# Scores of four heads on two row halves of TensorE, with unpadded pooled k and exponentials over two heads, in a fused pooling attention and MLP kernel

## Chip, cores, metric

One core of a Trainium2 chip. The metric is the device time of one execution in microseconds (us).

## The reference, cut to what matters

```python
# q, k, v: 8 batches, 8 heads, 576 positions, 64 channels
k_p = k.reshape(B, H, 72, 8, 64).mean(axis=3)          # pooled: 72 keys
v_p = v.reshape(B, H, 72, 8, 64).mean(axis=3)
attn = softmax(q @ k_p.T / 8)                          # 576 x 72 a head
x = (attn @ v_p)  -> (B, 576, 512)
u = x + lam * einsum('ts,bsd->btd', w_tok, alpha1 * x + beta1)
out = u + lam * (relu((alpha2 * u + beta2) @ w_ch1) @ w_ch2)   # 512 -> 2048 -> 512
```

The contraction of the scores is only 64 deep, half of TensorE's 128 rows. The last 64 of a head's 576 positions, "the remainder" below, are kept apart from the two halves of 256.

## The kernel before

The rows of all batches go through the MLP in nine blocks of 512. While block n runs on TensorE, the attention of batch n+1 is woven into it by a list of (position, work) pairs: `mlp_A` of hidden chunk j stands at position j (0 to 15), the 16 pieces of `mlp_B` at 16 to 31, and the attention's pieces have fractional positions between them. Every engine executes its share of the list in that order.

Scores are computed transposed (keys on the partitions of PSUM, the buffers that TensorE's matmuls write). `qT` has two sub-rows of 64 channels stacked on 128 partitions, so the kernel before pairs it with a pooled k that is zero in the other half:

```python
    def att_K(b, u, copy):
        # ... pooled k of four heads in ps_kp, 128 partitions (each half a copy) ...
        for a in range(2):
            rows = slice(64 * a, 64 * a + 64)
            (copy or ...)(out=kpT_pool[u][rows, a], in_=kp[rows])   # rest of kpT stays zero

    def att_S(b, h):
        u, r, hh = h // 4, h // 2 % 2, h % 2
        ET = ET_pool[h]
        for half in range(2):
            n0, n = 256 * half, 256 + 64 * half
            ps_sc = gp("ps_sc")                                      # one of 6 general PSUM buffers
            nc.tensor.matmul(out=ps_sc[0:SPG, 0:256], lhsT=kpT_pool[u][:, half, h % 4, :],
                             rhs=st["qT"][u][:, 2 * (h % 4):2 * (h % 4) + 2, :])
            if half:
                nc.tensor.matmul(out=ps_sc[0:SPG, 256:320], lhsT=kpT_pool[u][:, hh, h % 4, :],
                                 rhs=st["rem_qT"][:, :, h // 2::4].rearrange("p c i -> p i c"))
            nc.scalar.activation(out=ET[:, n0:n0 + n], in_=ps_sc[0:SPG, 0:n],
                                 func=AF.Exp, bias=0.0, scale=0.125)

    def att_AV(b, h):      # "AV": five matmuls, then on VectorE
        # ... av = ET[:, m0:m0+128].T @ [vp | 8], rec = 1/av[:, 64], x = av * rec ...

    def mlp_A(n, j):       # "a chunk": four 512-column matmuls, then on ScalarE
        # ... Hj = Relu(w1_j.T @ u + bias) ...
```

and the timetable of batch b from 2 on:

```python
        for h in range(8):
            at = 7.4 + 1.15 * h
            todo.append((at, lambda h=h: att_S(b, h)))         # scores, exponentials
            todo.append((at + 2.0, lambda h=h: att_AV(b, h)))  # two chunks later
```

The softmax here doesn't subtract the row's maximum and nothing guards it: scores larger than these inputs give would overflow.

## Time and profile before

| | kernel before |
|---|---|
| time, median | 364.95 us (3 runs, 364.85 to 365.48) |
| span of the profiled run | 363.5 us |
| TensorE busy | 96% |
| one batch's period in the steady part | 37.08 us |

The period is the mean distance of the first output addition of neighbouring blocks (from 102 to 288 us).

In all views PE is TensorE, PEld its weight loads, DVE VectorE, ACT ScalarE and POOL GpSimd. A line of a timeline gives start and length in us, then engine, source line, names and shapes, and in brackets the idle time before it and who ended it. `ps_s`, `ps_sc` and `ps_r` hold scores (`ps_r` those of the remainder), `ps_h` a chunk of the first MLP layer, `ps_ch` the second layer, `ps_tok` the token mixing.

```profile
L469 PE MATMUL ps_av<-vp,ET 72*128 72x66 f16 x256 | 18.0, 193 | 0.3 <-ACT wtT L299 0.3
L416 DVE CAST kpT<-ps_kp 64x288 bf16<-64x288 f32 x26 | 11.8, 455 | 9.4 <-PE ps_kp L409 5.2
```

TensorE (first figure) is busy for 37.00 of 37.00 us: it never waits. In the group lines the last column is the idle time of the engine just before these instructions, with who ended it; AV waited 0.3 us in the whole kernel, in the setup.

### The profile page before, as it was taken

To read this page: it belongs to the slowest core of one execution; us is meant where nothing else is said; L and a number is where in the kernel's file an instruction comes from. 1 tells how busy PE (TensorE), PEld (TensorE's weight loads), DVE (VectorE), ACT (ScalarE), POOL (GpSimd) and SP (SyncE) were. 2 spreads that over 40 slices of the span, in tenths; PEclk is the share of its full clock that TensorE was granted. 3 is DMA by queue.
4 is the path that set the end of the run, shared out by engine and by line. 5 is a ranking of instruction groups with operands and counts; after the bars stand their busy time and mean duration, and the time that the engine had idled before them with its cause. 6 is when DMAs were issued, how large, how long until landed. Compare 5 with 4: busy or idle time off the path is not lost.

```text
span 363.5 us, 5915 instructions
## 1 busy us (share of the span) xinstructions
PE 348.4 (96%) x2229; PEld 188.7 (52%) x2229; DVE 212.7 (59%) x456; ACT 153.9 (42%) x319; POOL 86.8 (24%) x99
## 2 busy tenths in 40 slices
PE   4888999899999999999999999999999999999994
PEld 1566666355644564456445644565456545545541
DVE  5574176669774878576857786677658761011011
ACT  2562995027800790069005910592049304703700
POOL 8469406252117000620053005300510000000000
PEclk9999999999999999999999999999999999999998
DMA  8999910998959872987198919872810032011012
GB/s 125 203 216 262 216 26 2 160 228 202 142 119 223 153 124 62 244 159 123 51 218 149 156 52 220 171 131 61 215 67 0 31 87 74 0 58 60 1 58 58
DMA packets 65886, 44.58 MB, mean 123 GB/s; under 512 B 32377, under 2 KB 57021, under 8 KB 65858
## 3 DMA queue, kind: packets, MB, share of 16 engines
q1 hardware_dynamic: 50480, 33.30, 38.3%
q0 software_dynamic: 15072, 10.76, 20.5%
q8 instruction: 17, 0.28, 0.3%
q10 hardware_dynamic: 306, 0.14, 0.2%
q14 instruction: 11, 0.09, 0.1%
HBM read 38.30 MB, written 9.44 MB: 131 GB/s over the span
## 4 chain that ended last, share of the span: by engine, by line
PE 90%; DVE 5%; ACT 1%; DMA 1%; issue 1%; ACTq 0%; DVEq 0%
PE ps_h L553 33%; PE ps_ch L571 33%; PE ps_tok L518 12%; PE ps_sc L450 4%; PE ps_av L469 2%; DVE x_tm L477 2%; PE ps_sc L453 1%; DMA vecs<-in_moe_alpha_dram 1%; PE ps_bc L278 1%; DVE kpT L416 1%; PE ps_kp L403 1%; DVE w L339 1%; PE ps_q L368 1%; DVE xs L484 0%; ACT u_fm L539 0%
## 5 line engine op out<-in xcount | busy, mean ns | idle before, releaser
L558 ACT ACTIVATE Hj<-ps_h,bias_cols 128x512 bf16<-128x512 f32 x144 | 98.7, 689 | 154.4 <-PE ps_h L553 153.5
L553 PE MATMUL ps_h<-u_fm,w 128*128 128x512 bf16 (+1 forms) x592 | 138.1, 374 | 1.3 <-ACT u_fm L539 1.1
L571 PE MATMUL ps_ch<-w,Hj 128*128 128x512 bf16 x576 | 134.2, 379 | 0.0
L571 PEld LDWEIGHTS <-Hj 128*128 128x128 bf16 x576 | 55.0, 98 | 62.0
L553 PEld LDWEIGHTS <-w 128*128 128x128 bf16 x592 | 63.4, 114 | 44.9 <-issue 1.8
L576 DVE TENSOR_TENSOR u_sb<-u_sb,ps_ch 128x512 f32<-128x512 f32 x36 | 24.7, 686 | 74.7 <-PE ps_ch L571 74.3
L518 PE MATMUL ps_tok<-xs,wtT 128*128 128x512 bf16 (+1 forms) x200 | 49.6, 379 | 1.8 <-DVE xs L484 1.8
L455 ACT ACTIVATE ET<-ps_sc 72x256 f16<-72x256 f32 (+1 forms) x128 | 44.5, 404 | 2.5 <-PE ps_sc L450 2.2
L520 DVE TENSOR_TENSOR u_sb<-x_tm,ps_tok 128x512 f32<-128x512 f32 (+1 forms) x40 | 27.5, 687 | 30.7 <-PE ps_tok L518 30.7
L477 DVE TENSOR_TENSOR x_tm<-ps_av,rec 128x320 f32<-128x320 f32 x64 | 31.4, 491 | 2.3
L147 POOL CAST rem_q<-rem_raw 128x256 bf16<-128x256 f32 x7 | 3.1, 437 | 123.3 <-DMA rem_raw<-in_q_dram 123.3
L518 PEld LDWEIGHTS <-wtT 128*128 128x128 bf16 (+1 forms) x200 | 19.2, 98 | 25.5 <-DVE xs L484 1.6
L522 DVE TENSOR_TENSOR u_bf<-u_sb,al_bc 128x512 bf16<-128x512 f32 (+1 forms) x38 | 29.0, 763 | 1.4
L438 DVE TENSOR_TENSOR v_u<-v_u 72x512 f32<-72x512 f32 (+1 forms) x48 | 28.3, 589 | 1.2
L450 PE MATMUL ps_sc<-qT,kpT 128*72 128x256 bf16 x128 | 25.4, 275 | 0.5 <-DVE kpT L416 0.4
L475 DVE RECIPROCAL rec<-ps_av 128x5 f32<-128x5 f32 x64 | 12.2, 191 | 18.6 <-PE ps_av L473 17.7
L469 PEld LDWEIGHTS <-ET 72*128 72x128 f16 x256 | 15.9, 98 | 11.9 <-issue 0.5
L162 POOL TENSOR_TENSOR k_raw<-k_raw 128x512 f32<-128x512 f32 x14 | 18.3, 1307 | 15.9 <-DMA k_raw<-in_k_dram 15.9
L164 POOL TENSOR_TENSOR k_bf<-k_raw 128x512 bf16<-128x512 f32 x14 | 19.4, 1386 | 1.1
L484 DVE TENSOR_TENSOR xs<-x_tm,lamal_bc 128x512 bf16<-128x512 f32 x26 | 18.3, 705 | 0.9
L469 PE MATMUL ps_av<-vp,ET 72*128 72x66 f16 x256 | 18.0, 193 | 0.3 <-ACT wtT L299 0.3
L416 DVE CAST kpT<-ps_kp 64x288 bf16<-64x288 f32 x26 | 11.8, 455 | 9.4 <-PE ps_kp L409 5.2
(111 smaller groups left out, 216.5 us busy)
## 6 DMA issues: line engine op xcount, KB each, us to landing
out_dram<-u_sb SPq DMA_DIRECT2D x32, 256.0 KB
k_raw<-in_k_dram SPq DMA_DIRECT2D x14, 512.0 KB
v_u<-in_v_dram SPq DMA_DIRECT2D x12, 512.0 KB
q_bf<-in_q_dram POOLq DMA_DIRECT2D x16, 256.0 KB, 6.7
w<-in_moe_w_ch_dram POOLq DMA_DIRECT2D x8, 512.0 KB, 10.9
v<-in_v_dram POOLq DMA_DIRECT2D x4, 256.0 KB, 6.8
out_dram<-u_sb SPq DMA_DIRECT2D x8, 128.0 KB
rem_raw<-in_q_dram SPq DMA_DIRECT2D x15, 64.0 KB
```

The lines of the kernel that those rows point to most:

```text
L438: nc.vector.tensor_tensor(out=t[:, :, 0:n], in0=t[:, :, 0:n], in1=t[:, :, n:2 * n], op=ALU.add)
L450: nc.tensor.matmul(out=ps_sc[0:SPG, 0:256], lhsT=kpT_pool[u][:, half, h % 4, :], rhs=st["qT"][u][:, 2 * (h % 4):2 * (h % 4) + 2, :])
L455: nc.scalar.activation(out=ET[:, n0:n0 + n], in_=ps_sc[0:SPG, 0:n], func=AF.Exp, bias=0.0, scale=0.125)
L469: nc.tensor.matmul(out=av[:, c, :], lhsT=ET[:, m0:m0 + 128], rhs=vp1[:, hh, :])
L477: nc.vector.tensor_tensor(out=x[:, :, dd:dd + D], in0=av[:, :, 0:64], in1=rec.unsqueeze(2).to_broadcast((P, 5, D)), op=ALU.mult)
L518: nc.tensor.matmul(out=ps_tok, lhsT=wtT[0:kk, at, t0:t0 + P], rhs=xs[0:kk, sc, :], start=(sc == 0), stop=(sc == 4))
L520: nc.vector.tensor_tensor(out=s["u"][p0:p1, :], in0=st1[b]["x"][p0:p1, c, :], in1=ps_tok[p0:p1, 0:DM], op=ALU.add)
L522: eng.tensor_tensor(out=s["u_bf"][p0:p1, :], in0=s["u"][p0:p1, :], in1=al2_bc[p0:p1, :], op=ALU.mult)
L553: nc.tensor.matmul(out=ps_h[:, t0:t1], lhsT=w1_of(cc, j), rhs=u_fm[n][:, cc, t0:t1], start=(cc == 0), stop=(cc == 3))
L558: nc.scalar.activation(out=t, in_=ps_h, func=AF.Relu, bias=bias_cols[:, j:j + 1], scale=1.0)
L571: nc.tensor.matmul(out=ps, lhsT=Hj[n, j][:, 128 * m:128 * m + 128], rhs=w2[j // 4][:, j % 4, :], start=(j == 0), stop=(j == NJ - 1))
L576: nc.vector.tensor_tensor(out=u, in0=u, in1=ps, op=ALU.add)
```

## The change

Its intent: the two halves of the rows hold separate matmuls, one with k on rows 0 to 63 and one on rows 64 to 127, and can run side by side, so that the zeros are no longer multiplied. Four heads form one group with twelve matmuls, into four general PSUM buffers and the two of the MLP output. Pooled k needs one copy without padding in place of two. An exponential then covers a 256-wide half of two heads at once (512 elements in place of 256 or 320). Batch 0 keeps the old form.

```diff
+        if b:
+            copy(out=kp_pool[u], in_=kp)
+            return
...
+    def att_S4(b, u):
+        lo = [psB.tile([P, DM], FP, tag="ch", bufs=2, name="ps_s") for _ in range(2)]
+        hi = [gp("ps_s") for _ in range(2)]
+        r = [gp("ps_r")[0:SPG, 0:128]... for _ in range(2)]
+        for i in range(4):                     # remainders of heads 0..3, halves in turn
+            a = i % 2
+            nc.tensor.matmul(out=r[a][:, i // 2], lhsT=kp[64 * a:64 * a + 64, i, :],
+                rhs=rest[64 * a:64 * a + 64, :, 2 * u + i // 2::4]...)
+        for i in (2, 3, 0, 1):
+            for a in range(2):                 # the pair on the two row halves
+                rows = slice(64 * a, 64 * a + 64)
+                nc.tensor.matmul(out=(hi if i > 1 else lo)[a][0:SPG, 256 * (i % 2):...],
+                    lhsT=kp[rows, i, :], rhs=qT[rows, 2 * i:2 * i + 2, :])
+        def exp(k):      # k = 0, 1: remainders; 2, 3: halves of heads 2, 3; 4, 5: of heads 0, 1
+            ...
...
-        for h in range(8):
-            at = 8.8 + 1.1 * h if first else 7.4 + 1.15 * h
-            lag = 3.3 if first else 2.0
-            todo.append((at, lambda h=h: att_S(b, h)))
-            todo.append((at + lag, lambda h=h: att_AV(b, h)))
...
+        for u in range(2):
+            at = (9.6 if first else 6.3, 12.8)[u]
+            todo.append((at, lambda u=u: att_S4(b, u)))
+            for k, dt in enumerate((0.1, 0.1, 0.2, 1.1, 2.1, 3.0)):
+                todo.append((at + dt, lambda k=k: st1[b]["exp"](k)))
+            lag = 0.9 if first else 0.0
+            for i, dt in ((2, 2.0), (3, 2.6), (0, 4.0), (1, 4.5)):
+                h = 4 * u + i
+                todo.append((at + lag + dt, lambda h=h: att_AV(b, h)))
```

More of the change, by code (lines that the diff above doesn't have):

```diff
@@ L231 @@
     load_wtok()
-    vp1_pool, kpT_pool, ET_pool = [], [], []
+    vp1_pool, kpT_pool, kp_pool, ET_pool = [], [], [], []
     for i in range(4):
@@ L241 @@
             kpT_pool.append(t)
-    for i in range(H):
-        t = const.tile([SPG, S + 64], F16, tag=f"ET_{i}", name=f"ET_{i}")
-        nc.vector.memset(t[:, S:], 1.0)
+            kp_pool.append(const.tile([P, 4, SPG], BF, tag=f"kp_{i}", name=f"kp_{i}"))
+    for i in range(2):
+        t = const.tile([SPG, 4, S + 64], F16, tag=f"ET_{i}", name=f"ET_{i}")
+        nc.vector.memset(t[:, :, S:], 1.0)
         ET_pool.append(t)
@@ L445, in att_S @@
         u, r, hh = h // 4, h // 2 % 2, h % 2
-        ET = ET_pool[h]
+        ET = ET_pool[u][:, h % 4]
         for half in range(2):
@@ L457, in att_S @@
         st["ET"][h] = ET
+    def att_S4(b, u):
+        st = st1[b]
+        qT, kp, rest = st["qT"][u], kp_pool[u], st["rem_qT"]
+        lo = [psB.tile([P, DM], FP, tag="ch", bufs=2, name="ps_s") for _ in range(2)]
+        hi = [gp("ps_s") for _ in range(2)]
+        r = [gp("ps_r")[0:SPG, 0:128].rearrange("p (h i) -> p h i", i=64) for _ in range(2)]
+        for i in range(4):
+            a = i % 2
+            nc.tensor.matmul(
+                out=r[a][:, i // 2], lhsT=kp[64 * a:64 * a + 64, i, :],
+                rhs=rest[64 * a:64 * a + 64, :, 2 * u + i // 2::4].rearrange("p c i -> p i c"))
+        for i in (2, 3, 0, 1):
+            for a in range(2):
+                rows = slice(64 * a, 64 * a + 64)
+                nc.tensor.matmul(
+                    out=(hi if i > 1 else lo)[a][0:SPG, 256 * (i % 2):256 * (i % 2) + 256],
+                    lhsT=kp[rows, i, :], rhs=qT[rows, 2 * i:2 * i + 2, :])
+        ET = ET_pool[u]
+        for i in range(4):
+            st["ET"][4 * u + i] = ET[:, i]
+        def exp(k):
+            if k < 2:
+                o, i = ET[:, k::2, 512:S], r[k]
+            else:
+                a, pair = k % 2, (hi, lo)[k // 2 - 1]
+                h = 2 if k < 4 else 0
+                o = ET[:, h:h + 2, 256 * a:256 * a + 256]
+                i = pair[a][0:SPG, :].rearrange("p (h i) -> p h i", i=256)
+            nc.scalar.activation(out=o, in_=i, func=AF.Exp, bias=0.0, scale=0.125)
+        st["exp"] = exp
     def att_AV(b, h):
@@ L694, in attention @@
                 todo.append((11.0 + 1.2 * u, lambda u=u: first_V(b, u, nc.scalar.copy)))
-        for h in range(8):
-            at = 8.8 + 1.1 * h if first else 7.4 + 1.15 * h
-            lag = 3.3 if first else 2.0
-            todo.append((at, lambda h=h: att_S(b, h)))
-            todo.append((at + lag, lambda h=h: att_AV(b, h)))
-            if h % 2:
-                eng = nc.gpsimd if first and h < 7 else nc.vector
-                todo.append((at + lag + 0.1, lambda h=h, eng=eng: att_X(b, h - 1, h + 1, eng)))
-            elif not first:
-                todo.append((0.2 + 1.0 * h, lambda h=h: att_V(b, h // 2)))
+        for u in range(2):
[7 more added lines that the diff above has]
+                todo.append((at + lag + dt, lambda h=h: att_AV(b, h)))
+                if i % 2:
+                    eng = nc.gpsimd if first and (u, i) != (1, 1) else nc.vector
+                    todo.append((at + lag + dt + 0.1,
+                                 lambda h=h, eng=eng: att_X(b, h - 1, h + 1, eng)))
+        if not first:
+            for hp in range(4):
+                todo.append((0.2 + 2.0 * hp, lambda hp=hp: att_V(b, hp)))
         for c in range(5):
```

## The prediction

> **What bounds the kernel now.** I read the page's busy shares first, then the slices, the groups, and finally the timeline of TensorE and ScalarE in one attention phase.
>
> ```profile
> PE 348.4 (96%) x2229; PEld 188.7 (52%) x2229; DVE 212.7 (59%) x456; ACT 153.9 (42%) x319; POOL 86.8 (24%) x99
> PE   4888999899999999999999999999999999999994
> ACT  2562995027800790069005910592049304703700
> L455 ACT ACTIVATE ET<-ps_sc 72x256 f16<-72x256 f32 (+1 forms) x128 | 44.5, 404 | 2.5 <-PE ps_sc L450 2.2
> L450 PE MATMUL ps_sc<-qT,kpT 128*72 128x256 bf16 x128 | 25.4, 275 | 0.5 <-DVE kpT L416 0.4
> ```
>
> TensorE is the bound: after the first few slices it is never below 9 tenths. ScalarE's 42% is an average that misleads: it is near 9 tenths in the slices where attention of batch b runs beside the first MLP layer of block b-1, and idle elsewhere. That phase is the one that the change rewrites. In it the PE timeline (start, length) of the kernel before reads:
>
> ```profile
> 162.16 0.38 PE L450 MATMUL ps_sc<-qT,kpT 128*72 128x256 bf16 x2
> 162.38 0.24 PE L453 MATMUL ps_sc<-rem_qT,kpT 128*72 128x64 bf16 x1
> 162.46 1.03 PE L553 MATMUL ps_h<-u_fm,w 128*128 128x512 bf16 x4
> 163.33 0.38 PE L450 MATMUL ps_sc<-qT,kpT 128*72 128x256 bf16 x2
> ```
>
> Starts are to be subtracted, as lengths include the pipeline. One head's scores cost 162.46 - 162.16 = 0.30 us of TensorE (two 256-column matmuls 0.11 apart, then 0.075 for the 64 strided columns); one hidden chunk of the MLP (four 512-column matmuls, "a chunk" below) costs 163.33 - 162.46 = 0.87. No idle time is printed here: from 65 us on the records show one TensorE gap above 0.1 us, about 0.4 us at 89 us. So anything removed from PE's stream counts in full, and so does any wait put into it.
>
> The ScalarE timeline of an attention phase:
>
> ```profile
> 87.83 0.69 ACT L558 ACTIVATE Hj<-ps_h,bias_cols 128x512 bf16<-128x512 f32 x1 [0.35 <-PE ps_h L553]
> 88.42 0.69 ACT L455 ACTIVATE ET<-ps_sc 72x256 f16<-72x256 f32 x2
> 89.00 0.69 ACT L558 ACTIVATE Hj<-ps_h,bias_cols 128x512 bf16<-128x512 f32 x1
> ```
>
> A Relu holds the engine 0.58 us (start to next start; 0.69 until its result), the two exponentials of a head 0.58 together. Relu must wait for its chunk: in the records it starts 0.20 to 0.25 us after the next matmul could start on PE. In the kernel before both exponentials of a head follow one Relu, and its attention-value matmuls (AV) come two chunks later, so they never waited.
>
> **What the Trainium skill says.** (1) "TensorE: Matmul & The Clock Gate", Part 3, Packing small matmuls: matmuls on different row groups run side by side, with starts some 4 ns apart. No run yet shows it here; it is the hope of the change. (2) "TensorEngine Tiling (Array Packing)", Key Properties: "Changing tiling mode (not just tile) drains the TensorE". The trace agrees and gives the price, at the places where 32-row weights (L428) come between full ones:
>
> ```profile
> 50.19 0.60 PE L426 MATMUL ps_v<-v,pool_v 128*72 128x256 f16 x4
> 50.72 0.40 PE L428 MATMUL ps_v<-v,pool_vr 32*72 32x256 f16 x2
> 51.05 0.41 PE L450 MATMUL ps_sc<-qT,kpT 128*72 128x256 bf16 x2
> ```
>
> Four 256-column matmuls should take 4 x 0.109 = 0.436 and take 0.53; two should take 0.218 and take 0.33. So in and out of the mode costs 0.09 + 0.11 = 0.20 us. (3) The same page, Gotcha 1: different row tiles must not share a PSUM bank at once; the change gives the halves separate banks, hence four banks and the two of the MLP output per group. (4) "ScalarE: Activation LUTs", What ACT_TABLE_LOAD costs: with immediate scale and bias 186 ns + 0.833 ns an element, neighbours overlapping by 93 ns. The trace has 0.37 us for an uncontended 256-wide exponential, 30 ns less than that; at its slope I estimate 0.59 us for 512 wide, 0.48 of it holding the engine.
>
> **The change, part by part** (batches 1 to 7, so 14 groups of four heads; batch 0 keeps the old form).
>
> 1. *Scores.* Before: 4 x 0.296 = 1.18 us a group. After: the same 12 matmuls, but as pairs on two row halves: two pairs of 0.075, four of 0.109, some 0.03 of skew, plus 0.20 for the mode, 0.82 us. Estimated gain 0.36 x 14 = **5.0 us**. Weight loads should stay hidden: after a mode switch the second 72-column load follows the first by only about 0.03 us.
>
> 2. *k without padding.* One copy of 128x288 on VectorE for two of 64x288 (455 ns each): 14 copies less, but VectorE is not the bound. At most the 0.4 us gap at 89 us goes (there a score matmul waits on this copy). The same group now needs the transposed q remainder about 1 us earlier, in batch 2 just as that transfer lands; I set the two off as zero.
>
> 3. *Exponentials.* Before 8 x 0.58 = 4.6 us of ScalarE per batch. After, per group two of 128 (about 0.16 each) and four of 512 (0.48): 2.24, so 4.5 per batch. No throughput is gained. What changes is order, and there lies the cost. The compiled streams, from batch 2 on, are:
>
> ```
> group 0  PE : S4 h7 h8 AV2 AV3 h9 h10 AV0 AV1
>         ACT: r r e2 Relu7 e3 Relu8 e4 Relu9 e5
> group 1  PE : S4 h13 h14 AV2 h15 AV3 B0 AV0 B1 AV1
>         ACT: r r Relu13 e2 e3 Relu14 e4 Relu15 e5
> ```
>
> (S4: scores of the group; h: a chunk; B: four matmuls of the second layer, as long as a chunk; e2, e3: the two column halves of heads 2 and 3; e4, e5: of heads 0 and 1; r: the remainders.) AV2's second matmul needs e3. Count from S4's end. Group 0: h7 done on PE at 0.87, Relu7 starts at 1.08, e3 at 1.66, its result at 2.25, seen by PE 0.05 later (the records' ScalarE-to-PE delay): 2.30. PE stands at AV2 at 2 x 0.87 + 0.03 = 1.77: **a wait of 0.53**. AV0 has the same pattern with Relu9 and e5: **0.53**. Group 1: e2 from 1.66, e3 from 2.14, result 2.73, 2.78 at PE: **1.0** at AV2; at AV0, with e5 behind Relu15, ready at 5.19 where PE stands at 4.81: **0.4**. Sum 2.5 us a batch, six batches: **+14.9 us**. Each of these was absent before, because an exponential did not stand behind a Relu that had itself to wait for the chunk just before the AV.
>
> 4. *Batch 1* runs on another timetable with 0.9 more lag: AV finds its exponentials ready. The first B takes a PSUM buffer that now holds scores of heads 0 and 1 until e4: +0.6. In return AV of its last head comes some 1.6 chunks earlier, which should take away the wait
>
> ```profile
> 65.44 0.82 PE L518 MATMUL ps_tok<-xs,wtT 128*128 128x512 bf16 x3 [1.11 <-DVE xs L484]
> ```
>
> which is 1.27 us by the starts: -1.2. Net -0.6.
>
> Sum: 364.95 - 5.0 + 14.9 - 0.6 = 374.3; I say **374.0 us**, 2.5% slower.
>
> **Rivals.**
> A. *The waits do not appear and the row halves work*: 364.95 - 5.0 - 1.2, about 359 us. For it: the timetable looks tuned by hand. Against: the instruction order leaves ScalarE idle between e2 and Relu7 while e3's scores lie ready, and PE has only one chunk of 0.87 to cover 0.2 + 0.58 + 0.59 + 0.05 = 1.42 us.
> B. *The halves do not overlap* (shared streaming of q, weight loads in a row, or the waits of their semaphores in between): a group costs 1.18 + 0.20, so +2.8 instead of -5.0; with the waits 382 us, without them 367 us. Nothing in the trace of before shows two row groups together, so this is open; the skill's measurements speak against it.
> C. *PSUM becomes the bound*: four of six general buffers go to one group, so the next chunks wait for Relu or exponentials to empty them. Following the six slots round, each was emptied at least as early as PE comes to it, h7's by about nothing (Relu6 ends as S4 ends). That could add 0.1 to 0.3 us a group, 1 to 4 us.
> D. *ScalarE as a throughput bound*: Relu 16 x 0.58 + 4.5 = 13.8 us in a phase of some 19 us on PE. Not reached; only its order matters.
>
> **Range and chances.** The waits are 24 differences of about 1.4 to 2.7 us against PE times; an error of 0.07 in each moves the sum by 1.7. The scores may be off by 3, C adds up to 4. That gives 366 to 380 as eight in ten. 2% slower is 372.25, 1.75 below the point; with a spread of some 4 and 7% for rival A: slower 0.62, within 2% 0.33, faster 0.05.
>
> **What the profile after would show.** Step 1: starts of the paired 256-column matmuls a few ns to 0.03 apart within a pair and 0.11 between pairs, S4 from start to next chunk near 0.82 (rival B: 1.3). Step 3: PE's idle time before AV with ScalarE's exponential as its releaser, about 2.5 us a batch from batch 2 on, PE's busy share falling to about 90%, and a 512-wide exponential near 0.59 us. Step 4: the 1.1 us wait at the first ps_tok gone. Rival C would show idle time before ps_h instead. I am wrong if AV waits are well under 0.4 us each (a Relu quicker off its chunk, or exponentials much shorter), or if S4 is far from 0.82.

## More of the kernel before

The busy time of the engines in one such period (the columns are the stretch, its length, then busy time and instructions of each engine, in the order PE, PEld, DVE, ACT, POOL, and last the granted clock, the DMA share and GB/s), and the groups for AV and the copies of pooled k:

```profile
160.00:197.00 37.00, 37.00 (x230) 19.83 (x229) 25.68 (x55) 15.31 (x33) 8.14 (x8) 1.00 0.66 139
```

## The result

| | before | changed |
|---|---|---|
| time, median | 365.16 us (4 runs) | 376.42 us (4 runs, 375.81 to 376.69) |
| ratio | | 1.0306, 95% interval 1.0288 to 1.0324 |
| span of the profiled run | 363.5 us | 374.1 us |
| TensorE busy | 96% | 93% |
| a batch's period in the steady part | 37.08 us | 38.79 us |

The ratio here and below is the mean time of one kernel's fast runs over that of the other's in the same rounds, so not quite the ratio of the medians. The change made the kernel 3% slower.

The page of the changed kernel, in the lines that answer to those of before:

```profile
PE 349.4 (93%) x2229; PEld 180.1 (48%) x2229; DVE 205.5 (55%) x438; ACT 151.8 (41%) x289; POOL 87.1 (23%) x99
PE   4988998998999989998999899999999999999994
PE 81%; ACT 10%; DVE 5%; issue 1%; DMA 1%; ACTq 0%; DVEq 0%
L495 ACT ACTIVATE ET<-ps_s 72x512 f16<-72x512 f32 x56 | 32.2, 588 | 0.0
L509 PE MATMUL ps_av<-vp,ET 72*128 72x66 f16 x256 | 20.5, 195 | 10.0 <-ACT ET L495 9.7
```

Between the eighth slice and the last TensorE never fell below 9 tenths before; now it drops to 8 four times there. The chain that ended last, 90% TensorE before, runs for a tenth of the span through ScalarE. And AV, which did not wait before, waits 10.0 us, of which 9.7 are ended by the exponential L495. This idle time is counted from the modelled end of the matmul before; by the starts, which decide, each wait is some 0.17 us longer.

One group of scores and what follows it on TensorE (group 0 of batch 3):

```profile
126.17 0.20 PE L410 MATMUL ps_kp<-pool_rem,rem_k 128*128 128x16 bf16 x2
126.30 0.35 PE L473 MATMUL ps_r<-rem_qT,kp 64*72 64x64 bf16 x4
126.48 0.60 PE L480 MATMUL ps_s<-qT,kp 64*72 64x256 bf16 x8
127.05 1.89 PE L593 MATMUL ps_h<-u_fm,w 128*128 128x512 bf16 x8
128.77 0.20 PE L509 MATMUL ps_av<-vp,ET 72*128 72x66 f16 x1
129.33 0.27 PE L509 MATMUL ps_av<-vp,ET 72*128 72x66 f16 x3 [0.36 <-ACT ET L495]
```

and on ScalarE at the same time:

```profile
126.89 0.42 ACT L495 ACTIVATE ET<-ps_r 72x128 f16<-72x128 f32 x2
127.21 0.59 ACT L495 ACTIVATE ET<-ps_s 72x512 f16<-72x512 f32 x1
128.11 0.69 ACT L598 ACTIVATE Hj<-ps_h,bias_cols 128x512 bf16<-128x512 f32 x1 [0.31 <-PE ps_h L593]
128.69 0.58 ACT L495 ACTIVATE ET<-ps_s 72x512 f16<-72x512 f32 x1
```

The twelve score matmuls take from 126.17 + 0.05 (the two small matmuls before them) to 127.05, 0.83 us for four heads where the kernel before needed 1.18: the part of the change that was its purpose works. But after its first 512-wide exponential ScalarE stands idle for 0.31 us with the next scores ready, because the next instruction in its order is a Relu whose chunk TensorE is only working on. The second exponential starts at 128.69 behind that Relu and ends at 129.27; AV's second matmul, which TensorE could have had at 128.80, starts at 129.33. In the second group of a batch two exponentials stand behind the Relu (batch 2):

```profile
98.27 0.20 PE L509 MATMUL ps_av<-vp,ET 72*128 72x66 f16 x1 [0.40 <-ACT ET L495]
98.75 0.27 PE L509 MATMUL ps_av<-vp,ET 72*128 72x66 f16 x3 [0.28 <-ACT ET L495]
```

By the starts of the matmuls, a batch waits 0.53 and 0.53 us in group 0 and 1.01 (in two steps) and 0.38 in group 1: 2.45 us, equal within 0.01 in all six batches from 2 to 7.

Where the 10.56 us between the two spans come from, by the distance of the blocks' first output additions:

| stretch | attention in it | changed against before |
|---|---|---|
| to the first output of block 0 | batches 0, 1 | +0.10 |
| block 0 to block 1 | batch 2 | +1.89 |
| blocks 1 to 6, five periods | batches 3 to 7 | +1.67, +1.77, +1.67, +1.77, +1.67 |
| after | none | +0.02 |

The timed difference, 11.26 us by the medians, is 0.7 larger than that of the spans: the two profiled executions were timed at 365.27 and 375.81 us, 10.54 apart, and the changed kernel's was the fastest of its four.

### The profile page after: what moved, and what is told of

It is laid out like the page before. It is cut to its first block, busy times and chain, and to the rows that moved or that the text cites.

```text
span 374.1 us, 5840 instructions
## 1 busy us (share of the span) xinstructions
PE 349.4 (93%) x2229; PEld 180.1 (48%) x2229; DVE 205.5 (55%) x438; ACT 151.8 (41%) x289; POOL 87.1 (23%) x99
## 4 chain that ended last, share of the span: by engine, by line
PE 81%; ACT 10%; DVE 5%; issue 1%; DMA 1%; ACTq 0%; DVEq 0%
PE ps_ch L611 31%; PE ps_h L593 28%; PE ps_tok L558 12%; ACT Hj L598 5%; ACT ET L495 4%; PE ps_av L509 2%; PE ps_s L480 2%; DVE x_tm L517 1%; DVE v_u L442 1%; PE ps_bc L279 1%; DMA vecs<-in_moe_alpha_dram 1%; PE ps_r L473 1%; PE ps_kp L404 1%; DVE w L340 1%; PE ps_q L369 1%
## 5 line engine op out<-in xcount | busy, mean ns | idle before, releaser
L593 PE MATMUL ps_h<-u_fm,w 128*128 128x512 bf16 (+1 forms) x592 | 134.2, 374 | 1.6 <-ACT u_fm L579 1.1
L495 ACT ACTIVATE ET<-ps_s 72x512 f16<-72x512 f32 x56 | 32.2, 588 | 0.0
L509 PE MATMUL ps_av<-vp,ET 72*128 72x66 f16 x256 | 20.5, 195 | 10.0 <-ACT ET L495 9.7
L509 PEld LDWEIGHTS <-ET 72*128 72x128 f16 x256 | 14.2, 97 | 25.7 <-ACT ET L495 18.7
L524 POOL TENSOR_TENSOR xs<-x_tm,lamal_bc 128x512 bf16<-128x512 f32 x6 | 9.5, 1591 | 23.6 <-DVE x_tm L517 23.2
L79 POOL DMA_DIRECT2D q_bf<-in_q_dram x16 | 12.4, 776 | 7.6 <-DVE q_bf L78 5.5
```

Of the source, the lines that this page charges most:

```text
L495: nc.scalar.activation(out=o, in_=i, func=AF.Exp, bias=0.0, scale=0.125)
L509: nc.tensor.matmul(out=av[:, c, :], lhsT=ET[:, m0:m0 + 128], rhs=vp1[:, hh, :])
L524: eng.tensor_tensor(out=xs[:, 0:4, cols], in0=x[:, 0:4, cols], in1=lamal_bc[:, cols].unsqueeze(1).to_broadcast((P, 4, D * (h1 - h0))), op= ...
L593: nc.tensor.matmul(out=ps_h[:, t0:t1], lhsT=w1_of(cc, j), rhs=u_fm[n][:, cc, t0:t1], start=(cc == 0), stop=(cc == 3))
```

## The experiments

Theory: the order on ScalarE makes AV wait; the row halves gain what they should; and the first two attention batches lose something of their own. Rivals: ScalarE's throughput or PSUM is the bound, so that a better order would only move the waits; the wide exponentials are to blame; the row halves gain nothing once the change of mode is paid. Each run was correct, and each is compared with runs of the kernel before in the same rounds.

### e1_exp_early: all exponentials ahead of the Relu

```diff
-            for k, dt in enumerate((0.1, 0.1, 0.2, 1.1, 2.1, 3.0)):
+            for k, dt in enumerate((0.1, 0.1, 0.2, 1.1, 2.1, 3.0) if first
+                                   else (0.1, 0.1, 0.11, 0.12, 0.13, 0.14)):
```

> From batch 2 on all six exponentials of a group stand on ScalarE ahead of the next chunk's Relu; nothing else changes. Theory (the order on ScalarE makes AV wait): the four waits of a batch in front of AV, 2.45 us in the trace of the changed kernel, vanish in six batches, so 376.4 - 14.7 = 361.7 us, and the profile shows no TensorE idle with the exponential as releaser from 80 us on. Rival (ScalarE's throughput, or PSUM emptied too late because Relus now come later): the waits move to ps_h and less than half of 14.7 us comes back, 369 us or more.

Measured: 362.62 us, ratio to before 0.9937 (0.9922 to 0.9952). 13.8 of the expected 14.7 us came back. The groups show the waits gone, and ScalarE's timeline the new order:

```profile
L509 PE MATMUL ps_av<-vp,ET 72*128 72x66 f16 x256 | 16.3, 193 | 0.3 <-ACT wtT L300 0.3
L558 PE MATMUL ps_tok<-xs,wtT 128*128 128x512 bf16 (+1 forms) x196 | 49.4, 379 | 2.5 <-DVE xs L524 2.2
```
```profile
161.81 0.42 ACT L495 ACTIVATE ET<-ps_r 72x128 f16<-72x128 f32 x2
162.12 2.05 ACT L495 ACTIVATE ET<-ps_s 72x512 f16<-72x512 f32 x4
164.03 2.63 ACT L598 ACTIVATE Hj<-ps_h,bias_cols 128x512 bf16<-128x512 f32 x4
```

The four 512-wide exponentials hold ScalarE from 162.12 to 164.03, so the next Relu starts about 1 us later than its chunk would allow. Three Relus then follow one another without a gap, 0.57 us from start to start against 0.87 of TensorE for a chunk, and before the fourth ScalarE is already idle for 0.08: the delay is made up without TensorE waiting. The spans differ by 12.85 us. Of the 1.85 that are missing there, some 1.4 us is the second line: in every batch the first token-mixing matmul now waits 0.12 or 0.35 us for VectorE, which the AV waits had hidden; another 0.5 was lost before the first output of block 0, where this edit changes nothing (six traces with the same timetable up to there have that output between 77.76 and 78.49 us, so this is scatter). The period is 36.59 us: 2.20 less than with the change's order, 0.49 less than before. The rival of throughput and PSUM falls: only the order was changed, and no new wait stands at `ps_h`.

### e2_av_later: leave the exponentials, move AV back

```diff
-            lag = 0.9 if first else 0.0
+            lag = 0.9 if first else 1.0
```

> The exponentials stay where the change put them, AV comes one chunk later on TensorE from batch 2 on. Theory: the waits of group 0 vanish (0.53 + 0.53), those of group 1 fall from 1.01 + 0.38 to about 0.15 + 0; but VectorE then has only one chunk left between the last AV and the first token-mixing matmul, which waits some 0.8 us. Per batch 2.45 - 0.15 - 0.8 = 1.5 us back, six batches 9 us: about 367.4 us. Rival (AV waits for something else than the exponential): the same 0.5 us waits in front of AV at its new place, 376 us.

Measured: 374.84 us, ratio 1.0268 (1.0253 to 1.0283); the expectation of 367.4 us was wrong. The waits in front of AV went as expected (none is left in group 0), but:

```profile
104.26 1.24 PE L558 MATMUL ps_tok<-xs,wtT 128*128 128x512 bf16 x5 [0.81 <-DVE xs L524]
...
137.85 1.02 PE L611 MATMUL ps_ch<-w,Hj 128*128 128x512 bf16 x4 [0.76 <-ACT ET L495]
```

The second line first: the first matmul of the second MLP layer takes a PSUM buffer that holds scores of heads 0 and 1 until the fifth exponential, which stands behind two Relus. With AV moved back, this matmul came earlier on TensorE, and waits 0.92 us by the starts; I had not counted it. The token mixing (first line) waits 0.98 and 1.21 us in turn by the starts, where 0.8 was expected. So the late exponential reaches TensorE by another way. Moving the consumer only moved the wait; moving the producer removed it.

### e3_exp_narrow: the change's order with 256-wide exponentials

```diff
-            nc.scalar.activation(out=o, in_=i, ...)                     # 72 x 2 x 256
+            for j in range(2):                                          # from batch 2 on
+                nc.scalar.activation(out=ET[:, h + j, 256 * a:256 * a + 256],
+                                     in_=pair[a][0:SPG, 256 * j:256 * j + 256], ...)
```

> From batch 2 on the 512-wide exponentials of two heads are taken apart into two of 256, at the same places in ScalarE's order. Theory (order, not width): an AV needs only its own head's half, ready about 0.2 us sooner, but the second half holds up the other head, so each batch's 2.45 us fall by about 0.4, six batches 2.7 us: 373.7 us. Rival (the wide exponential is what makes AV wait): most of the 14.7 us come back, 365 us or less. Other rival (two at once saves ScalarE time that matters): slower than 376.4 us.

Measured: 373.85 us, ratio 1.0236 (1.0219 to 1.0253), against 373.7 expected. Width is not the cause; two heads at once even costs 2.6 us in this order, as AV gets its own head's half later (with 256-wide exponentials it waits 0.43 us in group 0 by the starts, in place of 0.53).

### e9_narrow_early: both at once

The edits of e1_exp_early and e3_exp_narrow together.

> As e1_exp_early, with the wide exponentials from batch 2 on taken apart into 256-wide ones of one head each (as in e3_exp_narrow), so both changes at once. Theory: once the order is right, ScalarE has time to spare (20 exponentials a batch cost 4 x 0.16 + 16 x 0.27 = 5.0 us of it in place of 4.5), so two heads at once is worth nothing: 362.6 us within 0.5. Rival (two at once is needed once the exponentials stand in a block ahead of the Relu): 364 us or more.

Measured: 362.49 us, ratio 0.9931 (0.9914 to 0.9948): the same as e1_exp_early. With the right order the width of the exponentials is worth nothing either way.

### e4_padded: e1_exp_early without the row halves

```diff
-        if b:
-            copy(out=kp_pool[u], in_=kp)
-            return
...
-                out=r[a][:, i // 2], lhsT=kp[64 * a:64 * a + 64, i, :],
-                rhs=rest[64 * a:64 * a + 64, :, 2 * u + i // 2::4]...)
+                out=r[a][:, i // 2], lhsT=kpT_pool[u][:, a, i, :],
+                rhs=rest[:, :, 2 * u + i // 2::4]...)
...
-                    lhsT=kp[rows, i, :], rhs=qT[rows, 2 * i:2 * i + 2, :])
+                    lhsT=kpT_pool[u][:, a, i, :], rhs=qT[:, 2 * i:2 * i + 2, :])
```

> As e1_exp_early, but the scores of a group again with zero-padded k on all 128 rows, twelve full matmuls one after the other, so the row halves alone are undone (with the padded copies of k). Theory: a group costs 2 x 0.075 + 2 x 0.075 + 8 x 0.109 = 1.18 us in place of 0.82, so 0.36 x 14 = 5.0 us more than e1_exp_early, about 366.7 us. Rival (the row halves gain nothing, the mode switch eats it): same as e1_exp_early within 1 us.

Measured: 367.63 us, ratio 1.0073 (1.0058 to 1.0088), 5.0 us more than e1_exp_early as expected. On TensorE:

```profile
162.76 0.49 PE L470 MATMUL ps_r<-rem_qT,kpT 128*72 128x64 bf16 x4
163.08 1.04 PE L477 MATMUL ps_s<-qT,kpT 128*72 128x256 bf16 x8
163.96 1.24 PE L590 MATMUL ps_h<-u_fm,w 128*128 128x512 bf16 x4
```

A group takes 163.96 - 162.76 = 1.20 us on the full rows and 0.83 on the halves. In the steady part the period is 0.74 us longer, 0.37 a group, or 5.2 us for 14 groups. Nothing of the 5.0 is left over for the second copy of padded k on VectorE (also back in this run), and the row halves are worth 5 us net of the change of mode. It also shows that the grouped form alone, without the halves, is 0.7% slower than the kernel before.

### e5_split_mode: into the row-half mode twice a group

The four remainder matmuls and their two exponentials become a function of their own, from batch 2 on at position `at - 0.9`, one chunk ahead of the other eight.

```diff
             todo.append((at, lambda u=u: att_S4(b, u)))      # now only the eight
+            if not first:
+                todo.append((at - 0.9, lambda u=u: att_S4r(b, u)))   # the four remainders
```

> As e1_exp_early, but from batch 2 on the four remainder matmuls of a group stand one chunk ahead of its eight others, so that TensorE goes into the row-half mode and out of it twice a group in place of once; work and waits are otherwise the same. Theory (each change of mode costs about 0.2 us, in and out together, as the 32-row weights showed before): 12 groups x 0.2 = 2.4 us more than e1_exp_early, 365.0 us. Rival (the gap at the start and end of a group is something else, such as the first wait or the weight load): same as e1_exp_early within 0.7 us.

Measured: 366.88 us (8 runs, 366.24 to 368.74), ratio 1.0058 (1.0039 to 1.0076), 4.3 us more than e1_exp_early where 2.4 were expected. In the steady part the period is 0.47 us longer, 0.235 for each further visit to the mode, which is near the expected 0.2; five batches make 2.35 us. Another 1.57 us are lost in batch 2, 0.47 of them its own two visits. The rest is a wait: the remainders of group 0 start 2.08 us after the start of the last matmul before them, and what they wait for is the transfer that transposes the remainder of q:

```profile
87.97 0.35 PE L472 MATMUL ps_r<-rem_qT,kp 64*72 64x64 bf16 x4 [1.70 <-DMA rem_qT<-rem_q]
```

The same wait, 0.6 to 1.1 us, is in the changed kernel and in every run above and below up to e7_batch1_early. e4_padded's trace names the transfer too; in the other six the releaser printed is VectorE or ScalarE, as in the changed kernel:

```profile
87.52 0.35 PE L473 MATMUL ps_r<-rem_qT,kp 64*72 64x64 bf16 x4 [0.51 <-DVE v_u L442]
```

In all eight traces these matmuls start 0.135 to 0.136 us after the last semaphore event of that transfer, while the copy of pooled k had ended 0.68 to 1.19 us before, and the distances to VectorE's and ScalarE's last events vary from 0.02 to 0.97. So it is the transfer. Together 3.9 of the 4.3 us are found. This kernel's runs scatter: five at a clock of 0.998 to 0.999 took 366.24 to 367.05 us (median 366.66, 4.0 more than e1_exp_early), three at 0.993 to 0.995 took 367.89 to 368.74. The price of a visit is settled by the periods, not by the total.

### e7_batch1_early: the share of batch 1

```diff
-            ... (0.1, 0.1, 0.2, 1.1, 2.1, 3.0) if first else (0.1, 0.1, 0.11, ...)
+            ... (0.1, 0.1, 0.11, 0.12, 0.13, 0.14)
-                todo.append(((11.0, 11.2, 11.4, 16.6)[g], lambda g=g: scale_w2(g)))
+                todo.append(((11.0, 11.2, 11.4, 18.4)[g], lambda g=g: scale_w2(g)))
```

> As e1_exp_early, with the exponentials early in batch 1 too, and the scaling of the last quarter of the second weights (2.4 us of VectorE) behind batch 1's last AV work instead of between its AVs. Theory for the part of the time that the prediction missed (batch 1): in the trace of e1_exp_early TensorE waits 0.31 us for the first group's last exponentials to free a PSUM buffer, 0.62 us for the second's ahead of the first ps_ch, and 0.91 us for VectorE ahead of the first ps_tok. All three go: 362.6 - 1.8 = 360.8 us. Rival (batch 1 is held up by something further back, such as the setup copies on ScalarE): the waits move and under 0.7 us comes back.

Measured: 360.79 us, ratio 0.9878 (0.9861 to 0.9895), against 360.8 expected. In the trace the first output of block 0 comes 2.20 us sooner than in e1_exp_early (with the scatter of that output named there), and all later ones about 2.0 us, as group 0 of batch 2 now waits 0.2 us longer for the transfer. The three waits of batch 1, which the changed kernel shows as follows (the first line is the one left for the next run), are real and separate from those of the later batches:

```profile
48.82 1.89 PE L593 MATMUL ps_h<-u_fm,w 128*128 128x512 bf16 x8 [0.56 <-ACT Hj L598]
54.14 1.02 PE L480 MATMUL ps_s<-qT,kp 64*72 64x256 bf16 x8
58.94 1.02 PE L611 MATMUL ps_ch<-w,Hj 128*128 128x512 bf16 x4 [0.45 <-ACT ET L495]
65.55 0.81 PE L558 MATMUL ps_tok<-xs,wtT 128*128 128x512 bf16 x3 [0.76 <-DVE xs L524]
```

The second line's eight matmuls span 1.02 us where 0.60 is usual: one of them waits 0.31 us for the first group's last exponentials to leave its buffer.

### e6_best and e8_best2: the version that the runs point to

e6_best adds to e7_batch1_early:

```diff
+            late = ((2, 2.0), (3, 2.05), (0, 3.1), (1, 3.7))     # AVs of group 1, from batch 2 on
-            todo.append((8.3, setup_wtok_odd))
+            todo.append((18.5, setup_wtok_odd))
-                todo.append((0.2 + 2.0 * hp, lambda hp=hp: att_V(b, hp)))
+                todo.append(((6.2, 4.2, 10.2, 8.2)[hp] if b == 2 else 0.2 + 2.0 * hp, ...))
-            todo.append((-1.1, lambda: att_F(b, 2)))
+            todo.append((0.3, lambda: att_F(b, 2)))
```

> As e7_batch1_early, and: the AVs of the second group come earlier and further apart (so VectorE is done when token mixing starts), the odd setup copies of ScalarE move behind batch 1, and in batch 2 the pooled-k copy stands ahead of the v sums on VectorE with the remainder's transpose ahead of group 1's. From the trace of e1_exp_early: 0.12 to 0.35 us ahead of the first ps_tok in six batches (1.4 us), 0.73 us ahead of ps_h in batch 1, 0.7 us ahead of the scores of batch 2. Theory: 360.8 - 2.8 = 358.0 us. If batch 2 then waits for the transposed remainder instead, some 0.4 us more.

Measured: 358.76 us, ratio 0.9823 (0.9805 to 0.9840). The waits before token mixing, before `ps_h` in batch 1 and before group 0 of batch 2 are gone; for the last the earlier transfer counts, issued at 81.65 us ahead of the second of q's transposes, in place of 85.09 behind it in the changed kernel. A new wait of 0.81 us stands in group 1 of batch 2, for VectorE. e8_best2 changes one thing, the positions of the v sums in batch 2 from (6.2, 4.2, 10.2, 8.2) to (4.2, 2.2, 8.2, 6.2).

> As e6_best, with the v sums of batch 2 on VectorE one before the first pooled-k copy, one after it, one after the second, the last after the next chunk. In e6_best the last v sum (1.4 us) stood between two AVs on VectorE and the second group's scores waited 0.81 us for the PSUM buffers that VectorE freed late. Theory: that wait goes, 358.76 - 0.8 = 358.0 us. Rival (VectorE simply has too much to do in batch 2): the wait comes back at the first group or stays, 358.7 us.

Measured (4 runs): 358.11 us, against 365.11 us of the kernel before in the same rounds, ratio 0.9808 (0.9793 to 0.9823). This version beats both: 1.9% faster than before, 4.9% than the changed kernel by the medians. Its longest waits of TensorE in the list of who waited for whom are all in the setup of the first 60 us, before the steady part:

```profile
PE ps_bc L279 <- DMA vecs<-in_moe_alpha_dram: 3.8, 1, 3.8
PE ps_warm L548 <- DVE warm L203: 1.4, 1, 1.4
PE ps_h L593 <- ACT u_fm L579: 1.1, 2, 0.7
PE ps_tok L558 <- DVE xs L524: 0.9, 1, 0.9
```

Its period is 36.29 us, 0.79 less than before, where the scores were to give 2 x 0.36 = 0.72.

## Why the prediction was right

The prediction gave 374.0 us (366 to 380) and slower; measured were 376.42. Its mechanism held, and the time missed is mainly in one term, step 4. Two readings of its lines were loose: the eighth slice of TensorE is an 8, and from 65 us on there are two gaps, as the wait at 65.44 that step 4 quotes is one of them. And two signs missed: TensorE's busy share fell to 93%, not about 90%, and the wait at the first `ps_tok` did not go (step 4).

- **Step 1, the scores**: predicted 0.82 us a group, measured 0.83 in group 0 and 0.81 in group 1. The two matmuls of a pair start 3 to 4 ns apart, in group 0 of batch 2 some 25 ns; from pair to pair it is about 0.109 us in all groups. e4_padded confirms the gain as 5.0 us in time. Rival B falls.
- **Step 2, unpadded k**: off the path, as e4_padded shows. Its last sentence named the right two effects in batch 2 and set them off as zero. The 0.4 us gap at 89 us went, and in its place group 0 of batch 2 waits about 0.6 us for the transposed remainder of q, as it feared (e5_split_mode shows that it is this transfer). Batch 2 therefore added 1.89 us, not the 1.7 of the others.
- **Step 3, the order of exponentials**: predicted waits 0.53, 0.53, 1.0, 0.4; measured 0.53, 0.53, 1.01, 0.38. The wide exponential was estimated at 0.59 us and took 0.588. The waits as it worked them out add up to 2.45 us a batch, 14.7 in six, not quite the 14.9 that it carried on. With the gain on the scores the 14.9 give +1.76 us a batch; the periods show +1.71. e1_exp_early shows that the order causes it.
- **Step 4, batch 1**: this is the term that was mis-sized. With its share of step 1 it should have brought 1.3 us and brought nothing (+0.10 us at the first output; that output scatters by 0.7 between traces, but the waits of batch 1 named here, less the gain on the scores, also add up to +0.1). The wait of the first `ps_ch` was predicted as 0.6 and is 0.61. But three things were missed. The wait for VectorE before token mixing was to vanish and is 0.92 of its 1.27 us: AV comes earlier, yet the scaling of the second weights (2.4 us) still stands between the last AVs on VectorE. A group's scores wait 0.31 us for a PSUM buffer. And the first chunk after the first group waits 0.63 us, its buffer's Relu being behind two setup copies; the kernel before lost 0.39 there. e7_batch1_early and e6_best give these back when their causes are moved, several at a time. This is 1.4 us of the 2.2 by which the predicted change of the time (+9.05) was too small against 11.26. The rest is the 0.7 us between spans and timed runs, 0.3 lost in rounding the sum of 374.3 down to 374.0, and 0.1 of batch 2, with the steady batches 0.25 on the other side.
- **Rival A** would have been right with another order: e1_exp_early gives 362.62, not the 359 named, since the waits of batch 1 and batch 2 stay and token mixing waits 1.4 us in all. **Rival C** is the 0.31 us in batch 1, and the 0.63; from batch 2 on it was not seen in the changed kernel, but it appears in the runs: at the two MLP output buffers in e2_av_later, where the slots had not been followed, and in group 1 of batch 2 in e6_best (0.81 us).

## What to carry to other kernels

Where an engine executes in strict order, ask of each instruction not what it costs but what it stands behind: an exponential whose scores were ready was held for about 1 us (from about 127.7 to 128.69 in batch 3) because a Relu in front of it waited for TensorE's current chunk, and TensorE waited 0.53 us in turn. Work whose inputs are ready goes ahead of work that must wait for the bound engine; the delayed work caught up by itself, since ScalarE needs 0.57 us for a Relu whose chunk takes TensorE 0.87. And when a gain is real but the time does not show it, move the producer forward before moving the consumer back: here the latter mostly sent the wait on, to the next shared buffer and to VectorE. And look behind the named releaser: the wait of batch 2 was put down to VectorE, and only the two runs in which it was longest showed the transfer.

## What the Trainium skill lacked or had wrong

- "TensorEngine Tiling (Array Packing)", Key Properties, says that a change of tiling mode drains TensorE, but not what it costs. Here 0.09 us on the way in and 0.09 on the way out with 32 rows, and after each the second matmul comes 0.03 late, 0.24 in all (the prediction's 0.20 leaves the last 0.03 out); and 0.235 us for each further visit to the 64-row mode (e5_split_mode).
- "TensorE: Matmul & The Clock Gate", Part 2, Back-to-back issue gap, has about 131 ns a matmul at 512 columns as the sustained pace of weight load and matmul pairs. Every stream of such pairs here runs at 216 ns, which is the page's own isolated figure. For 64 columns that figure would be 29 ns; the 64 columns of the remainder, strided in memory, took 75 ns, where the 64 contiguous ones of pooled k's matmuls took 29. "SBUF — State Buffer" says that such reads pay a penalty, but no page gives its size.
- The same page, LDWEIGHTS, gives P / 1.2 ns, so 60 ns for 72 columns. After a change of mode the second 72-column load started 32 ns after the first and the matmul behind it came 27 ns late, about half; that this spacing is the load's own time is not shown.
- "ScalarE: Activation LUTs", What ACT_TABLE_LOAD costs, gives 186 ns + 0.833 ns an element with immediate scale and bias. The exponentials take 267 ns at 128 and 587 at 512 elements in the changed kernel and 368 at 256 in the kernel before (medians), 25 to 31 ns less; in e1_exp_early, one behind the other, the 512-wide ones take 602.
